# The last two operations of four weights' conversion, and the additions to k's sums, move from VectorE to GpSimd

## The chip, the cores and the metric

The kernel runs on one core of a Trainium2 chip. The metric is device time in microseconds (us) of one execution. The core has five engines that run their own instruction lists in order and wait for each other through semaphores: TensorE (PE in the rows), VectorE (DVE), ScalarE (ACT), GpSimd (POOL) and SyncE (SP, which here only issues transfers). An engine that waits for a semaphore holds everything that stands behind the waiting instruction in its list.

## The reference

Three layers follow each other: linear attention, a two-layer network, and a mixture of eight experts whose gate is balanced by eight Sinkhorn rounds.

```
k_s = exp(k - max(k, axis=seq));  k_s = k_s / (sum(k_s, axis=seq) + 1e-9)
q_s = exp(q - max(q, axis=dim));  q_s = q_s / (sum(q_s, axis=dim) + 1e-9)
x   = q_s @ (k_s^T @ v)                    # 4 batches, 8 heads, 576 tokens, 64 dims
x   = maximum(0.01*h, h) @ w_out,  h = x @ w_in        # 2304 x 512 -> 2048 -> 512
P   = exp(x @ w_gate - max), 8 rounds of row and column normalisation
out = sum_e P[:, e] * (relu(x @ w1[e]) @ w2[e])
```

The first network's two weights come as 64-bit floats. The kernel reads each as two 32-bit words and makes from them a high and a low fp32r part, so that three fp32r matmuls stand for one product of fp32 accuracy.

## The kernel before

Tokens lie in 18 tiles of 128 (`q_task(i)`, i from 0), which are grouped into 6 blocks of 384 (`x_task(bl)`, `first`, `second`). The hidden layer of the first network is cut into 16 units of 128 columns; a unit's weights have two halves, (u, 0) for the first matrix and (u, 1) for the second. `prep_half(u, half)` converts one half: it takes 512 numbers per partition through seven operations on VectorE and two on ScalarE, and the last two (lines 169 and 170) make the low part: L169 subtracts the high part, L170 adds the contribution of the low word and writes the result into `wa` (units 0 to 3), where the matmuls read it. In the kernel before, units 4 to 7 already do these two lines on GpSimd; all others do them on VectorE.

`k_task(b, hp)` handles batch b and pair of heads hp: VectorE takes the maximum (L269), ScalarE the exponential with its sum over the tokens in `sm` (L271), TensorE transposes (L279), ScalarE copies (L281), VectorE adds EPS to the sum (L282, 128 x 1) and takes the reciprocal (L283), TensorE multiplies by v, and ScalarE scales the product by the reciprocal (L295). `q_task` alternates between engines: maximum on VectorE (L305), subtraction on GpSimd (L307), exponential on ScalarE (L309), sum, addition and reciprocal on VectorE (L311 to L313), multiplication on GpSimd (L314), transposes on TensorE (L319) and a copy on ScalarE (L320). `x_task` multiplies the block by the batches' products (`px`), and writes the high part (ScalarE, L345) and the low part (VectorE, L346) of x into `xs`; `first(0)`, the matmuls `ph`, is the first use of them.

Everything is issued from a table of half steps: the tasks are generators, `at(t, task)` says in which half step one begins, and each half step advances all that are active by one piece. Steps below 0 lie ahead of `first(0)`. The lists of TensorE, ScalarE, GpSimd and SyncE are in the order in which the program text issues them, since they are set to be manual; only VectorE's list is put in order by the scheduler of the framework. The loads of the raw weights go round three buffers, so a load waits until L170 has read the buffer that it overwrites:

```
    for t, (u, half) in zip((-12, -8, -5, -1, 3, 6, 8, 11), halves0):
        at(t, prep_half, u, half)
```

`halves0` is (0,0), (1,0), (0,1), (1,1), (2,0), (3,0), (2,1), (3,1).

Of the kernel before, what the change touches and what calls it, by code (L numbers as in the profile page):

```python
# [16 lines left out]
EPS = 1e-9  # L17
# [5 lines left out]
def kernel(  # L23
# [26 lines left out]
    nc = tc.nc  # L50
# [12 lines left out]
    PU = 4  # L63
# [26 lines left out]
    def r32(ap):  # L90
        return ap.bitcast(F32)
# [26 lines left out]
    def unit(u):  # L118

        if (u // PU) % 2 == 0:  # L120
            t = wa[:, u % PU * US : (u % PU + 1) * US]
        else:
            t = later["wb"][:, u % PU * US : (u % PU + 1) * US]
        return t.rearrange("p (h l n) -> p h l n", h=2, l=2)
# [11 lines left out]
    def load(free=False):  # L136
        if queue[0][0] >= 2 * PU and not free:
            return
        u, half = queue.pop(0)
        t = raw_t[u, half] = later["ml"].tile([P, 2 * DM], F32, tag="raw", name=f"raw{u}_{half}", bufs=later["raws"])  # L140
        nc.sync.dma_start(
            t.bitcast(U32), wm[u, :, half * DM : (half + 1) * DM].bitcast(U32)
        )

    def prep_half(u, half):


        raw = raw_t.pop((u, half)).bitcast(U32).rearrange("p (n t) -> p n t", t=2)
        w0, w1 = raw[:, :, 0], raw[:, :, 1]
        hi, lo = unit(u)[:, half, 0, :], unit(u)[:, half, 1, :]  # L150
        a = later["ml"].tile([P, DM], U32, tag="ca", name=f"ca{u}_{half}", bufs=6 - later["raws"] if later["raws"] == 3 else 1)
        af, ef = a.bitcast(F32), w1.bitcast(F32)
        nc.scalar.activation(af, ef, AF.Abs)
        yield
        nc.vector.tensor_scalar(af, af, EXP_MIN, EXP_MAX, op0=ALU.max, op1=ALU.min)
        nc.vector.tensor_scalar(
            a, a, 3, 0x3FFFFFFF, op0=ALU.logical_shift_left, op1=ALU.bitwise_and
        )
        nc.vector.scalar_tensor_tensor(
            a, w1, 0xC0000000, a, op0=ALU.bitwise_and, op1=ALU.bitwise_or  # L160
        )
        yield
        nc.scalar.copy(hi, af)
        nc.vector.tensor_scalar(w1, a, 0xFF800000, None, op0=ALU.bitwise_and)
        nc.vector.scalar_tensor_tensor(ef, w0, 2.0**-52, ef, op0=ALU.mult, op1=ALU.mult)
        yield

        eng = nc.gpsimd if PU <= u < 2 * PU else nc.vector
        eng.tensor_tensor(af, af, r32(hi), op=ALU.subtract)  # L169
        eng.tensor_tensor(lo, af, ef, op=ALU.add)  # L170
        ready.add((u, half))
        if u < 2 * PU:
            load()
# [17 lines left out]
    def bank(name):  # L191
        pool, tag = spare[0]
        spare.append(spare.pop(0))
        return pool.tile([P, 512], F32, tag=tag, name=name)
# [8 lines left out]
    def mm(o, a, b, start, stop, **more):  # L203
        nc.tensor.matmul(o, a, b, start=start, stop=stop, **more)  # L204
# [60 lines left out]
    def k_task(b, hp):  # L265
        k = k_t.pop((b, hp))
        nm = att.tile([P, 1], F32, tag="knm", name=f"knm{b}_{hp}")
        sm = att.tile([P, 1], F32, tag="ksm", name=f"ksm{b}_{hp}", bufs=4)
        nc.vector.tensor_reduce(nm, k, axis=AX.X, op=ALU.max, negate=True)  # L269
        yield  # L270
        nc.scalar.activation(k, k, AF.Exp, bias=nm, accum_out=sm)  # L271
        yield PE_NEXT
        ke = att.tile([P, SC, P], F32, tag="ke", name=f"ke{b}_{hp}")
        for c0 in range(0, SC, 4):
            pt = bank(f"pk{b}_{hp}_{c0}").rearrange("p (c d) -> p c d", d=P)
            m = min(4, SC - c0)
            for c in range(c0, c0 + m):
                r = min(P, S - c * P)
                nc.tensor.transpose(pt[:r, c - c0, :], k[:, c * P : c * P + r], ident)  # L279
            r = min(P, S - (c0 + m - 1) * P)  # L280
            nc.scalar.copy(ke[:r, c0 : c0 + m, :], pt[:r, :m, :])  # L281
        nc.vector.tensor_scalar_add(sm, sm, EPS)  # L282
        nc.vector.reciprocal(sm, sm)  # L283
        yield PE_NEXT
        v = v_t.pop((b, hp))
        pt = bank(f"pkv{b}_{hp}")[:, :P]
        for c in range(SC):
            r = min(P, S - c * P)
            mm(pt, ke[:r, c, :], v[:r, c, :], c == 0, c == SC - 1)

        assert b < 2 or all(("x", i) in ready for i in range(-(-(b - 1) * S // P)))
        ready.add(("kv", b, hp))
        for j in range(2):
            js = slice(j * D, (j + 1) * D)
            nc.scalar.mul(kv[b % 2][js, hp, js], pt[js, js], sm[js])  # L295
# [981 lines left out]
    for b, tk, tv, ts in (  # L1277
# [4 lines left out]
    ):  # L1282
        for hp, t in enumerate(ts):
            if tk is not None:
                at(tk[hp], k_load, b, hp)
                at(tv[hp], v_load, b, hp)
            at(t, k_task, b, hp)
# [9 lines left out]
    for t, (u, half) in zip((-12, -8, -5, -1, 3, 6, 8, 11), halves0):  # L1297
        at(t, prep_half, u, half)
# [7 lines left out]
    for t, (f, half) in zip((26, 28, 32, 34, 36, 41, 43, 45), halves):  # L1306
        at(t, prep_half, PU + f, half)
    at(H2 + 2, open_raws)
    for ph in range(1, NPH - 1):
        for t, (f, half) in zip((5, 11, 16, 21, 28, 33, 39, 44), halves2):  # L1310
            at(H2 * ph + t - 3, load, True)
            at(H2 * ph + t, prep_half, PU * (ph + 1) + f, half)
# [108 lines left out]
```

## Time and profile before

| | before |
|---|---|
| median of 3 runs | 1951.55 us (1951.3 to 1952.67) |
| the profiled execution | 1952.44 us, of which the profile's span is 1950.7 us |
| TensorE busy | 1920.2 us (98%) |
| VectorE busy | 1550.5 us (79%) |
| ScalarE busy | 835.9 us (43%) |
| GpSimd busy | 754.8 us (39%) |
| TensorE's granted clock, mean | 0.995 of full |

Times in the rows are counted from the span's start. "Idle before" in square brackets is how long the engine had done nothing ahead of an instruction, and the arrow names what released it. Instructions of one line that follow each other are merged in the list in order of time, with their number behind an x.

### The profile page before, as it was taken

The numbers are of one execution on the slowest core, as the hardware profiler recorded it, in microseconds if no ns is written. First come the engines' busy times: TensorE is split into PE (matmuls) and PEld (weight loads), VectorE is DVE, ScalarE is ACT, GpSimd is POOL, SyncE is SP. The second block draws the span as 40 slices with busy tenths as digits, with TensorE's granted clock in tenths as the row PEclk, the third lists the DMA queues.
The fourth block names the chain that finished last, engine by engine and source line by source line (L and its number), as shares of the span: only waits on it lengthen the run. The fifth ranks groups of instructions, "written<-read, shape, count | busy, mean of one in ns | idle before, by whom it ended". The sixth has DMA issues, their size and how long they took to land.

```text
span 1950.7 us, 31219 instructions
## 1 busy us (share of the span) xinstructions
PE 1920.2 (98%) x10835; PEld 1862.6 (95%) x10835; DVE 1550.5 (79%) x2285; ACT 835.9 (43%) x1518; POOL 754.8 (39%) x560
## 2 busy tenths in 40 slices
PE   7999999999999999999999999999999999999998
PEld 6999999999888999899999999999999999999998
DVE  7866767756888787778897888888898888888886
ACT  6754434445544444333444333333344333333333
POOL 4134223123324333135434444445443444444442
PEclk8999999999999999999999999999999999999999
DMA  6502768657787988888788988788888888888884
GB/s 241 170 12 65 247 213 266 214 184 237 254 303 288 335 289 307 310 295 259 239 275 271 320 282 264 249 271 259 260 251 255 272 261 260 259 260 242 271 261 146
DMA packets 279450, 483.59 MB, mean 248 GB/s; under 512 B 23376, under 2 KB 62688, under 8 KB 279264
## 3 DMA queue, kind: packets, MB, share of 16 engines
q1 hardware_dynamic: 278496, 480.04, 74.6%
q0 software_dynamic: 800, 1.57, 0.5%
q8 instruction: 88, 1.44, 0.3%
q14 instruction: 66, 0.54, 0.1%
HBM read 356.14 MB, written 128.52 MB: 248 GB/s over the span
## 4 chain that ended last, share of the span: by engine, by line
PE 53%; DVE 4%; issue 0%; ACT 0%; DMA 0%; POOL 0%; SPq 0%; ACTq 0%; DVEq 0%; POOLq 0%
PE e L204 27%; PE pa L204 7%; PE pc L204 7%; PE pd L204 7%; PE pb L204 4%; DVE xs L539 1%; DVE c L944 1%; DVE mo_t L814 1%; DVE mo_t L800 1%; DVE wa L539 0%; PE po L914 0%; DVE acc L843 0%; DMA wa<-d 0%; POOL acc L838 0%; ACT xs L538 0%
## 5 line engine op out<-in xcount | busy, mean ns | idle before, releaser
L838 POOL TENSOR_TENSOR acc<-acc,acc 128x384 f32<-128x384 f32 x222 | 336.7, 1517 | 331.1 <-ACT acc L837 319.6
L204 PE MATMUL e<-xs,wb_t 128*128 128x384 f32 x1728 | 326.9, 335 | 4.2 <-DVE acc L843 2.5
L204 PEld LDWEIGHTS e<-xs,wb_t 128*128 128x128 f32 x1728 | 302.2, 188 | 4.9 <-DVE acc L843 2.9
L204 PE MATMUL e<-wa,wb_t 128*128 128x384 f32 x1464 | 278.3, 335 | 1.6 <-DVE wa L539 1.6
L204 PEld LDWEIGHTS e<-wa,wb_t 128*128 128x128 f32 x1464 | 256.5, 188 | 1.9 <-DVE wa L539 1.9
L814 POOL TENSOR_TENSOR mo_t<-mo_t 128x768 f32<-128x768 f32 x72 | 139.3, 1934 | 307.3 <-DVE mo_t L800 282.2
L837 ACT COPY acc<-e 128x384 f32<-128x384 f32 x222 | 106.5, 480 | 303.9 <-PE e L204 302.8
L539 DVE TENSOR_TENSOR wa<-mo_t,wa 128x768 fp32r<-128x768 f32 (+2 forms) x176 | 192.8, 1108 | 17.3 <-ACT wa L538 17.3
L539 DVE TENSOR_TENSOR xs<-mo_t,xs 128x768 fp32r<-128x768 f32 x145 | 164.9, 1153 | 25.5 <-ACT xs L538 25.5
L204 PE MATMUL pa<-xs,wb_t 128*128 128x384 f32 x888 | 181.4, 338 | 1.1 <-ACT c L997 1.1
L204 PE MATMUL pd<-xs,wb_t 128*128 128x384 f32 x888 | 178.9, 335 | 1.4 <-DVE xs L539 1.4
L538 ACT CAST wa<-mo_t 128x768 fp32r<-128x768 f32 (+2 forms) x176 | 143.8, 839 | 81.8 <-DVE mo_t L814 60.7
L204 PE MATMUL pc<-xs,wb_t 128*128 128x384 f32 x888 | 177.8, 334 | 0.0
L843 DVE TENSOR_TENSOR acc<-e,acc 128x384 f32<-128x384 f32 x284 | 145.4, 547 | 32.0 <-PE e L204 17.5
L204 PE MATMUL e<-wb_t,xs 128*128 128x512 f32 x720 | 167.7, 390 | 0.0
L204 PEld LDWEIGHTS e<-wb_t,xs 128*128 128x128 f32 x720 | 134.7, 188 | 27.3
L204 PEld LDWEIGHTS pa<-xs,wb_t 128*128 128x128 f32 x888 | 154.1, 188 | 6.7 <-ACT c L997 5.9
L204 PEld LDWEIGHTS pd<-xs,wb_t 128*128 128x128 f32 x888 | 155.7, 188 | 2.2 <-DVE xs L539 2.0
L204 PEld LDWEIGHTS pc<-xs,wb_t 128*128 128x128 f32 x888 | 156.0, 188 | 0.1
L538 ACT CAST xs<-mo_t 128x768 fp32r<-128x768 f32 x145 | 117.8, 835 | 84.0 <-DVE mo_t L814 64.4
L814 DVE TENSOR_TENSOR mo_t<-mo_t 128x768 f32<-128x768 f32 x80 | 146.0, 1826 | 0.0
L800 DVE SCALAR_TENSOR_TENSOR mo_t<-c,mo_t 128x768 f32<-128x768 f32 (+1 forms) x152 | 131.8, 888 | 2.5
(177 smaller groups left out, 3219.1 us busy)
## 6 DMA issues: line engine op xcount, KB each, us to landing
wb_t<-d SPq DMA_DIRECT2D x1050, 256.0 KB, 3.4
d<-wa SPq DMA_DIRECT2D x20, 1792.0 KB, 9.6
d<-wb_t SPq DMA_DIRECT2D x56, 512.0 KB, 4.5
mo_t<-in_w SPq DMA_DIRECT2D x40, 512.0 KB, 7.3
raw<-in_wm SPq DMA_DIRECT2D x32, 512.0 KB, 5.3
d<-wa SPq DMA_DIRECT2D x15, 1024.0 KB, 5.1
d<-xs SPq DMA_DIRECT2D x13, 768.0 KB, 4.9
d<-wb_t SPq DMA_DIRECT2D x9, 1024.0 KB, 5.0
```

What stands on the lines that cost most here:

```text
L204: nc.tensor.matmul(o, a, b, start=start, stop=stop, **more)
L538: nc.scalar.copy(hi, a)
L539: return lambda: nc.vector.tensor_tensor(lo, a, r32(hi), op=ALU.subtract)
L800: nc.vector.scalar_tensor_tensor(o, p, 0.0, r, op0=ALU.max, op1=ALU.mult)
L814: eng.tensor_tensor(raw_q(o), raw_q(x), raw_q(y), op=ALU.subtract)
L837: nc.scalar.copy(t, bk[b])
L838: nc.gpsimd.tensor_tensor(c22, c22, t, op=ALU.add)
L843: return nc.vector.tensor_tensor(a, bk[b], a, op=ALU.add)
L944: add = lambda o, x, y: nc.vector.tensor_tensor(o, x, y, op=ALU.add)
```

## The change

Two engines are exchanged. `prep_half` gives lines 169 and 170 of units 0 to 3 to GpSimd as well, and `k_task` gives its addition of EPS to GpSimd. The reciprocal behind that addition stays on VectorE.

```
@@ -165,7 +165,7 @@
-        eng = nc.gpsimd if PU <= u < 2 * PU else nc.vector
+        eng = nc.gpsimd if u < 2 * PU else nc.vector
         eng.tensor_tensor(af, af, r32(hi), op=ALU.subtract)
         eng.tensor_tensor(lo, af, ef, op=ALU.add)
@@ -279,7 +279,7 @@
-        nc.vector.tensor_scalar_add(sm, sm, EPS)
+        nc.gpsimd.tensor_scalar_add(sm, sm, EPS)
         nc.vector.reciprocal(sm, sm)
```

Sixteen instructions of L169 and L170 (eight halves) and sixteen of L282 change the engine. The lists of TensorE, ScalarE and SyncE stay as they were. The names in the lists below: `ca1_0` is the work tile of half (1, 0), `ksm1_3` the sum of batch 1 and pair of heads 3, `qmx2` and `qsm2` the maximum and the sum of token tile 2, `px0_2` the third product of token block 0; the number behind the last underscore is a buffer's.

The first place is GpSimd's list from the second instruction of token tile 0 to the multiplication of tile 1, some 14 to 20 us into the span.

```order
 L314 TENSOR_TENSOR acc0_79<-acc0_79,qsm0_208 128x512
+L169 TENSOR_TENSOR ca0_0_210<-ca0_0_210,wa_86 128x512
+L170 TENSOR_TENSOR wa_86<-ca0_0_210,raw0_0_177 128x512
 L307 TENSOR_TENSOR acc0_79<-acc0_79,qmx1_242 128x512
+L282 TENSOR_SCALAR ksm0_2_220<-ksm0_2_220 128x1
 L307 TENSOR_TENSOR acc0_79<-acc0_79,qmx2_282 128x512
+L282 TENSOR_SCALAR ksm0_3_240<-ksm0_3_240 128x1
 L314 TENSOR_TENSOR acc0_79<-acc0_79,qsm1_243 128x512
```

The pair of half (0, 0) now stands ahead of the subtractions of tiles 1 and 2, and the two additions stand between and behind those. At the same place VectorE's list is this now:

```order
L313 RECIPROCAL qsm0_208<-qsm0_208 128x8
L305 TENSOR_REDUCE qmx2_282<-acc0_79 128x8
L283 RECIPROCAL ksm0_2_220<-ksm0_2_220 128x1
L283 RECIPROCAL ksm0_3_240<-ksm0_3_240 128x1
L311 TENSOR_REDUCE qsm1_243<-acc0_79 128x8
```

The two reciprocals, which stood behind VectorE's own additions, now wait for GpSimd's, and the sum of tile 1 still stands behind them.

The second place is GpSimd's list some 30 to 38 us into the span, with the pair of half (1, 0).

```order
 L314 TENSOR_TENSOR acc1_80<-acc1_80,qsm3_313 128x512
+L169 TENSOR_TENSOR ca1_0_315<-ca1_0_315,wa_86 128x512
+L170 TENSOR_TENSOR wa_86<-ca1_0_315,raw1_0_195 128x512
 L307 TENSOR_TENSOR acc1_80<-acc1_80,qmx5_395 128x512
+L282 TENSOR_SCALAR ksm1_1_352<-ksm1_1_352 128x1
 L314 TENSOR_TENSOR acc1_80<-acc1_80,qsm4_355 128x512
 L314 TENSOR_TENSOR acc1_80<-acc1_80,qsm5_396 128x512
+L282 TENSOR_SCALAR ksm1_2_417<-ksm1_2_417 128x1
+L169 TENSOR_TENSOR ca0_1_419<-ca0_1_419,wa_86 128x512
+L170 TENSOR_TENSOR wa_86<-ca0_1_419,raw0_1_197 128x512
 L307 TENSOR_TENSOR acc2_81<-acc2_81,qmx6_473 128x512
 L307 TENSOR_TENSOR acc2_81<-acc2_81,qmx7_476 128x512
```

The addition for `ksm1_1` stands behind a pair and a subtraction now. The next instruction of this list, which is new too, is the addition for `ksm1_3`; it stands behind the pair of half (0, 1) and two subtractions. VectorE's list at the second place:

```order
 L311 TENSOR_REDUCE qsm4_355<-acc1_80 128x8
 L155 TENSOR_SCALAR ca0_1_419<-ca0_1_419 128x512
+L283 RECIPROCAL ksm1_1_352<-ksm1_1_352 128x1
 L312 TENSOR_SCALAR qsm4_355<-qsm4_355 128x8
+L156 TENSOR_SCALAR ca0_1_419<-ca0_1_419 128x512
+L313 RECIPROCAL qsm4_355<-qsm4_355 128x8
```

The reciprocal of `ksm1_1` moved behind the first operation of half (0, 1), and the sums of tile 4 stand behind it. VectorE's list at the third place, some 38 to 43 us into the span, before:

```order
L346 TENSOR_TENSOR xs_85<-px0_0_479,xs_85 128x384
L346 TENSOR_TENSOR xs_85<-px0_1_483,xs_85 128x384
L283 RECIPROCAL ksm1_2_417<-ksm1_2_417 128x1
L169 TENSOR_TENSOR ca0_1_419<-ca0_1_419,wa_86 128x512
L282 TENSOR_SCALAR ksm1_3_449<-ksm1_3_449 128x1
L170 TENSOR_TENSOR wa_86<-ca0_1_419,raw0_1_197 128x512
L346 TENSOR_TENSOR xs_85<-px0_2_514,xs_85 128x384
L346 TENSOR_TENSOR xs_85<-px0_3_518,xs_85 128x384
```

And in the changed kernel:

```order
L346 TENSOR_TENSOR xs_85<-px0_0_479,xs_85 128x384
L346 TENSOR_TENSOR xs_85<-px0_1_483,xs_85 128x384
L283 RECIPROCAL ksm1_2_417<-ksm1_2_417 128x1
L283 RECIPROCAL ksm1_3_449<-ksm1_3_449 128x1
L346 TENSOR_TENSOR xs_85<-px0_2_514,xs_85 128x384
L346 TENSOR_TENSOR xs_85<-px0_3_518,xs_85 128x384
```

The pair and the addition are gone from between the four L346, and the reciprocal of `ksm1_3` has come to stand ahead of the last two.

## Rows read from the trace of the kernel before

**Rows 1.** Busy us by stretch: PE, PEld, DVE, ACT, POOL, clock, DMA share, GB/s.
```profile
0.00:45.00 45.00, 31.38 (x173) 26.22 (x174) 33.22 (x78) 30.23 (x72) 18.16 (x23) 0.85 0.64 232
30.00:40.00 10.00, 7.04 (x41) 4.92 (x40) 10.00 (x23) 8.70 (x21) 6.72 (x7) 1.00 0.17 53
45.00:130.00 85.00, 85.00 (x540) 80.17 (x539) 63.13 (x142) 58.33 (x136) 22.95 (x21) 1.00 0.36 120
```

**Rows 2.** In order of time, all engines, 14 to 22 us: start, us, instruction.
```profile
14.00 0.69 DVE L169 TENSOR_TENSOR ca<-ca,wa 128x512 f32<-128x512 f32 x1
...
14.60 0.20 DVE L313 RECIPROCAL qsm<-qsm 128x8 f32<-128x8 f32 x1
...
14.95 1.37 POOL L314 TENSOR_TENSOR acc<-acc,qsm 128x512 f32<-128x512 f32 x1 [8.15 <-ACT kv L295]
...
16.28 2.04 POOL L307 TENSOR_TENSOR acc<-acc,qmx 128x512 f32<-128x512 f32 x2
...
18.01 0.69 DVE L311 TENSOR_REDUCE qsm<-acc 128x8 f32<-128x512 f32 x1 [1.68 <-ACT acc L309]
...
18.94 0.20 DVE L313 RECIPROCAL qsm<-qsm 128x8 f32<-128x8 f32 x1
...
21.07 0.78 ACT L271 ACTIVATE k<-k,knm 128x576 f32<-128x576 f32 x1 [3.09 <-DVE knm L269]
...
21.99 1.33 PE L279 MATMUL pk<-ident,k 128*128 128x128 f32 x5 [3.67 <-ACT k L271]
```

**Rows 3.** In order of time, VectorE, 28 to 43 us.
```profile
28.32 0.69 DVE L311 TENSOR_REDUCE qsm<-acc 128x8 f32<-128x512 f32 x1 [1.35 <-ACT acc L309]
...
30.27 0.19 DVE L313 RECIPROCAL qsm<-qsm 128x8 f32<-128x8 f32 x1
...
32.85 0.16 DVE L312 TENSOR_SCALAR qsm<-qsm 128x8 f32<-128x8 f32 x1
...
37.88 1.01 DVE L346 TENSOR_TENSOR xs<-px,xs 128x384 fp32r<-128x384 f32 x2
...
38.89 1.53 DVE L169 TENSOR_TENSOR ca<-ca,wa 128x512 f32<-128x512 f32 x1
40.34 0.14 DVE L282 TENSOR_SCALAR ksm<-ksm 128x1 f32<-128x1 f32 x1
...
41.79 1.01 DVE L346 TENSOR_TENSOR xs<-px,xs 128x384 fp32r<-128x384 f32 x2
```

**Rows 4.** In order of time, TensorE, 42 to 49 us.
```profile
42.48 0.63 PE L319 MATMUL pq<-ident,acc 128*128 128x128 f32 x4 [0.58 <-DVE xs L346]
...
44.79 4.41 PE L204 MATMUL ph<-xs,wa 128*128 128x384 f32 x24
```

**Rows 5.** L169 and L170 on GpSimd: ns min/median/max, first and last start.
```profile
L169 POOL TENSOR_TENSOR ca<-ca,wb_t x8: 1290/1620/1759, 142.1 to 189.1; 128x512 f32<-128x512 f32 x8
L170 POOL TENSOR_TENSOR wb_t<-ca,raw x8: 1299/1363/1372, 143.9 to 190.8; 128x512 fp32r<-128x512 f32 x8
```

**Rows 6.** In order of time, GpSimd, from the start and at 30 and 36 us.
```profile
0.35 0.10 POOL L1410 MEMSET const-uint8-127<- 128x1 uint8 x1
...
30.60 1.04 POOL L314 TENSOR_TENSOR acc<-acc,qsm 128x512 f32<-128x512 f32 x1 [2.07 <-DVE ksm L283]
...
36.37 1.05 POOL L314 TENSOR_TENSOR acc<-acc,qsm 128x512 f32<-128x512 f32 x1 [1.47 <-DVE qsm L313]
```

**Rows 7.** In order of time, ScalarE, TensorE and VectorE at 64 to 69 us.
```profile
64.45 0.62 ACT L163 CAST wa<-ca 128x512 fp32r<-128x512 f32 x1
...
66.99 2.54 PE L204 MATMUL ph<-xs,wa 128*128 128x384 f32 x12
...
67.41 1.15 DVE L346 TENSOR_TENSOR xs<-px,xs 128x384 fp32r<-128x384 f32 x2
```

**Rows 8.** Busy us by stretch, columns as in rows 1, around the clock's fall.
```profile
20.00:21.00 1.00, 0.00 (x0) 0.00 (x0) 1.00 (x3) 0.00 (x0) 1.00 (x2) 1.00 1.01 407
21.00:22.00 1.00, 0.01 (x1) 0.01 (x1) 1.00 (x2) 0.93 (x3) 0.33 (x1) 0.64 1.03 409
```

More of the change, by code (lines that the diff above doesn't have):

```diff
@@ L166, in prep_half @@
         yield
-        eng = nc.gpsimd if PU <= u < 2 * PU else nc.vector
+        eng = nc.gpsimd if u < 2 * PU else nc.vector
         eng.tensor_tensor(af, af, r32(hi), op=ALU.subtract)
@@ L281, in k_task @@
             nc.scalar.copy(ke[:r, c0 : c0 + m, :], pt[:r, :m, :])
-        nc.vector.tensor_scalar_add(sm, sm, EPS)
+        nc.gpsimd.tensor_scalar_add(sm, sm, EPS)
         nc.vector.reciprocal(sm, sm)
```

## The prediction

> **What bounds the kernel now.** I read the busy times by stretch first. In the first 45 us TensorE works 31.38 us; in the 85 us behind them it works all 85.00 [rows 1]. So the kernel is a start, in which TensorE waits for the attention's small operations, and then a dense row of matmuls. Whatever moves the first matmuls of the network (`ph`) moves everything behind them by as much, and a saving on VectorE later than that is hidden by TensorE's own work. The question is what the change does to the start.
>
> Then I read the start in order of time. From 14 to 22 us [rows 2] a chain goes round: VectorE's L313 of tile 0, GpSimd's L314 and two L307, ScalarE's exponential, VectorE's L311 of tile 1 (18.01, after 1.68 us idle), maxima, and at 21.07 ScalarE's exponential of batch 1, for which ScalarE had waited 3.09 us and TensorE 3.67. GpSimd is in that chain, though it is idle most of the time. From 30 to 40 us VectorE is busy all 10.00 us [rows 1]: the list runs from L311 at 28.32 to the last L346, which begin at 41.79 [rows 3]. TensorE waits for just those L346 ahead of `pq` at 42.48, and `ph` begins at 44.79 [rows 4], 3.0 us behind their begin.
>
> **The pieces and their prices.** Moved are eight pairs of L169 and L170 and sixteen L282. On VectorE a lone L169 took 0.69 us [rows 2]; beside busy GpSimd the pair took from 38.89 to 41.79, 2.9 us [rows 3]. On GpSimd the same lines, in the same shape, took 1.29 to 1.76 and 1.30 to 1.37 us [rows 5]; with 0.1 us between them (my estimate; L170 waits for L169) a pair is 2.7 to 3.2 us. I take 2.7 where VectorE stands still beside it and 2.9 where it works. The Trainium skill ("GPSIMD Engine Reference", section "Instruction dispatch") puts the floor of a two-input operation at some 2.5 cycles per element, with 1.2 GHz in section "Specifications": 512 elements would be an estimated 1.07 us, a pair 2.1, and three pairs on the path below would make the sum some 1.8 us smaller. The row of these very lines, 1.29 us at the least, decides, so I do not use it.
>
> An L282 on GpSimd has no row. Nearest below is a memset of 128 x 1 at 0.10 us [rows 6]; above I take twice VectorE's 0.14 [rows 3], the ratio that the pair has. I use 0.10, since size hardly matters here, and keep 0.28 for the range. From GpSimd to VectorE a hop of 0.15 (L313 ends at 14.80, L314 begins at 14.95) and a reciprocal of 0.20 [rows 2] follow: 0.35 together.
>
> What matters more is the place in the lists. Both engines keep their order: VectorE's reciprocals now wait for an L282 that stands in GpSimd's list behind a pair and one or two L307, and VectorE holds all that stands behind the reciprocal. Four places, each reckoned from the one ahead:
>
> *First, 18 us.* L313 of tile 0 no longer has an L169 ahead (0.60 us), but a reciprocal has moved ahead of it and its wait for L312 lies open: I count 0.4 of the 0.6, so L314 begins at 14.55 instead of 14.95 [rows 2]. It takes 1.05 [rows 6], to 15.6; the pair 2.7, to 18.3; L307 1.02 (half of 2.04), L282 0.10, L307 1.02, L282 0.10, to 20.55. With 0.35 the L311 of tile 1, which stands behind both reciprocals, begins at 20.9 instead of 18.01: 2.9 us late. ScalarE and TensorE, which waited for what follows anyway, are late by as much.
>
> *Second, 33 us.* L314 of tile 3 stood at 30.60 [rows 6]. It is 2.9 late, but VectorE needs 0.93 us from L311 to L313 where nothing lies between (18.01 to 18.94) and needed 1.95 here (28.32 to 30.27, with L169, L170 and an L282 between): 1.0 comes back. So 32.5; L314 1.04, pair 2.9, L307 1.02, L282 0.10: 37.55; with 0.35 it is 37.9. VectorE's L312 of tile 4, behind that reciprocal, stood at 32.85 [rows 3]: 5.1 late.
>
> *Third, 42 us.* L314 of tile 5 stood at 36.37 [rows 6]; with 5.1, and 0.3 since an L164 now stands ahead of its sum, it begins at 41.75. L314 1.05, L282 0.10, pair 2.7, two L307 2.04, L282 0.10: 47.75; with 0.35 it is 48.1. The last two L346 stood at 41.79: 6.3 late. What VectorE saves, the 2.9 us of the pair ahead of them, is inside that, as idle time. `ph` begins at 51.1 instead of 44.79.
>
> *Fourth, 68 us.* From `ph` on TensorE has no gaps to give back. Half (2, 0) gets its high part at 64.45 plus 0.62; a pair of 2.7, L282 and 0.35 end at 68.25, and the L346 behind that reciprocal stood at 67.41 [rows 7]: 0.85 late. The `ph` that reads them began at 66.99 and takes about 0.19 us for each of its 12 matmuls; it comes to this part at the eighth, 68.3, and the first L346 was done at about 67.95, so 0.35 is spare: 0.5 late.
>
> Past that, waits of the same kind fall on sums and halves with microseconds to spare, and I count them at nothing. The cover there is TensorE's own row of matmuls; if it were gone, the pair of half (1, 1), which the second set of matmuls behind `ph` reads, would be late next.
>
> **The sum.** 6.3 + 0.5 = 6.8 us. Against the profiled execution, 1952.44 us (a span of 1950.7 and 1.7 around it), that is 1959.2; the median of the runs shown is 0.9 lower, 1951.55, and so I predict 1958.3 us. Low ends (pairs of 2.6, 0.6 gained at the first place, the fourth hidden) take off 1.2, and if TensorE, whose transposes at 21.99 ran below the full clock [rows 8], is back at it earlier in the later start, up to 1.2 more: 4.4. High ends (pairs of 3.2: 1.3; five L282 of 0.28 on the path: 0.9; nothing gained at the first place: 0.4; no spare at the fourth: 0.35) give 9.8. The forecast's own range is 1955.9 to 1961.4.
>
> **The rivals.** *VectorE's relief wins.* From 28.32 to 42 us VectorE is the bound, and the change takes from it 1.0 us, 2.9 us and some 0.6 us of L282: 4.5 in all, 1947.0. That needs every L282 to be done before VectorE comes to the reciprocal; it decides where a pair and the L307 beside it take less time than VectorE has work ahead of the reciprocal. Against it: at the second place GpSimd needs 5 us behind L314, and VectorE's list has only three larger operations there. For it: GpSimd was busy 18.16 of the first 45 us [rows 1]. One in ten.
>
> *The first delay is hidden.* If batch 1's exponential at 21.07 really stood for a transfer, 2.9 us drop out: 3.9 are left, 1955.4. Against it the row names VectorE's maximum as what ended that wait [rows 2]. 15 in 100.
>
> *The clock falls.* At the second place TensorE loses its work: the products of block 0 need tile 2's copy, which stands on ScalarE behind the exponential of tile 5, and that waits for the delayed L307. By the times above TensorE has a gap of some 3 us ahead of the products and of 2 ahead of `pq`. Before, a gap of 3.67 us ended with the granted clock at 1.00 from 20 to 21 us and 0.64 from 21 to 22 [rows 8], on its way from 2.4 to 1.2 GHz. If it falls again just ahead of `ph`, the first two sets of `ph`, 4.41 us [rows 4], take up to twice as long: 2 to 4.4 us more, 3 in the middle, 1961.3. The Trainium skill ("TensorE: Matmul & The Clock Gate", section "What's actually happening") calls the lower level the default, which activity releases; by that rule the gaps speak for the fall, and the trace agrees with it for its one gap of 3.67 us. But the gaps here are shorter and broken by transposes. 17 in 100.
>
> *It does nothing that can be measured*, as the start is covered by something that I do not see: 3 in 100.
>
> **The numbers.** The forecast keeps 55 in 100. What a measurement of this kernel can tell from no change is about 0.2%, 3.9 us. Slower by more than that: the forecast, the clock, and a little of the case with the hidden delay, 0.74. Faster by more: 0.09 of the first rival. The same: 0.17, most of the hidden delay. The range leaves out the faster case and the nothing, and the far end of the clock's: 1953.5 to 1963.5.
>
> **What would show it.** In the profile after: `ph` begins at about 51 us; TensorE's busy time behind it is unchanged; VectorE stands idle ahead of three L283 (ahead of 21, 38 and 48 us), released by GpSimd's L282; GpSimd's pairs last 2.7 us and more, and the L307 of tiles 1, 5, 6 and 7 are late by 2 to 8 us. The forecast is wrong if those idle times are absent, if the pairs take near 2.1 us, or if TensorE, warm and late, catches up later in waits that I have taken for its own.

## The result and the profile after

The changed kernel takes 1961.99 us (median of 4 runs, 1961.11 to 1962.85) against 1951.42 us (4 runs, 1951.06 to 1952.67) before: 0.54% slower, with an interval of the ratio from 1.0042 to 1.0066. It was forecast at 1958.3 us, slower, with a range of 1953.5 to 1963.5 us. The profiled execution took 1961.37 us, its span 1959.6 us.

The busy times by stretch of the kernel after, which answer to [rows 1]:

```profile
0.00:45.00 45.00, 29.00 (x145) 24.43 (x146) 25.44 (x60) 27.30 (x64) 24.26 (x34) 0.81 0.61 222
45.00:130.00 85.00, 80.89 (x493) 74.31 (x492) 55.43 (x118) 56.30 (x133) 39.29 (x42) 0.98 0.38 125
```

In the start TensorE works 2.4 us less than before and VectorE 7.8 us less; GpSimd works 6.1 us more. The line that was not expected is the second: in the 85 us behind the start TensorE is no longer busy throughout, but 80.89 us, and its clock is at 0.98. (The start is longer now, so some of these 4.1 us still belong to it; from 55 to 140 us TensorE is busy 82.40 of 85 us, where it was busy all 85.00 before.)

The start in order of time, all engines, kernel after; first the place that answers to [rows 2]:

```profile
13.84 1.04 POOL L314 TENSOR_TENSOR acc<-acc,qsm 128x512 f32<-128x512 f32 x1 [3.43 <-DVE qsm L313]
...
14.84 1.27 POOL L169 TENSOR_TENSOR ca<-ca,wa 128x512 f32<-128x512 f32 x1
...
18.79 0.16 DVE L283 RECIPROCAL ksm<-ksm 128x1 f32<-128x1 f32 x1 [4.55 <-POOL ksm L282]
...
20.21 0.16 DVE L283 RECIPROCAL ksm<-ksm 128x1 f32<-128x1 f32 x1 [1.25 <-POOL ksm L282]
20.29 0.67 DVE L311 TENSOR_REDUCE qsm<-acc 128x8 f32<-128x512 f32 x1
...
24.20 1.11 PE L279 MATMUL pk<-ident,k 128*128 128x128 f32 x4 [6.94 <-ACT k L271]
```

VectorE stands idle for 4.55 and 1.25 us ahead of two L283 until GpSimd's L282 are done, which stand behind the pair and the L307. L311 of tile 1 comes at 20.29 instead of 18.01, the transposes at 24.20 instead of 21.99. At the prediction's second place VectorE is held for 2.47 us, and L312 of tile 4 comes at 36.90 instead of 32.85:

```profile
36.82 0.16 DVE L283 RECIPROCAL ksm<-ksm 128x1 f32<-128x1 f32 x1 [2.47 <-POOL ksm L282]
36.90 0.15 DVE L312 TENSOR_SCALAR qsm<-qsm 128x8 f32<-128x8 f32 x1
```

The same at the end of the start, which answers to [rows 3, 4]:

```profile
46.97 0.21 POOL L282 TENSOR_SCALAR ksm<-ksm 128x1 f32<-128x1 f32 x1
...
47.21 0.16 DVE L283 RECIPROCAL ksm<-ksm 128x1 f32<-128x1 f32 x1 [4.66 <-POOL ksm L282]
...
47.29 1.00 DVE L346 TENSOR_TENSOR xs<-px,xs 128x384 fp32r<-128x384 f32 x2
...
47.98 0.63 PE L319 MATMUL pq<-ident,acc 128*128 128x128 f32 x4 [1.51 <-DVE xs L346]
...
50.28 4.41 PE L204 MATMUL ph<-xs,wa 128*128 128x384 f32 x24
```

The last two L346 come at 47.29 instead of 41.79, `ph` at 50.28 instead of 44.79: 5.5 us late. VectorE's waits from 0 to 130 us (us in total, times, longest) say how much it stood for this. The second row, waits for a transfer of k, is taken up with the single pairs below:

```profile
DVE ksm L283 <- POOL ksm L282: 21.5, 8, 5.1
DVE knm L269 <- DMA k<-in_kt: 7.9, 3, 2.8
```

Behind `ph`, again in order of time, the delay grows twice more by little. The first row is the fourth place of the prediction:

```profile
74.26 1.16 PE L204 MATMUL ph<-xs,wa 128*128 128x384 f32 x5 [0.17 <-DVE xs L346]
...
85.52 0.16 DVE L283 RECIPROCAL ksm<-ksm 128x1 f32<-128x1 f32 x1 [1.23 <-POOL ksm L282]
...
87.41 1.57 PE L204 MATMUL pkv<-v,ke 128*128 128x128 f32 x10 [0.49 <-DVE hh L221]
```

`ph` is held for 0.17 us at 74.26 and reads the low part late; its followers are 5.9 us late instead of 5.5. A hold of L283 at 85.52 makes the subtraction for `hh` (L221) late, and TensorE waits for that: 6.6 us. Then, with the pair of half (3, 1):

```profile
108.17 0.16 DVE L283 RECIPROCAL ksm<-ksm 128x1 f32<-128x1 f32 x1 [5.12 <-POOL ksm L282]
...
110.25 0.55 DVE L221 TENSOR_TENSOR hh<-ph,hh 128x384 fp32r<-128x384 f32 x1
...
110.86 0.77 PE L279 MATMUL pk<-ident,k 128*128 128x128 f32 x5 [1.94 <-DVE hh L221]
...
111.46 2.24 PE L204 MATMUL pkv<-v,ke 128*128 128x128 f32 x10
...
113.63 3.13 PE L204 MATMUL ph<-xs,wa 128*128 128x384 f32 x12
```

Here two things happen. VectorE stands 5.12 us at L283, comes late to L305 and L221, and TensorE, whose transposes need what L221 sets free, has its largest gap behind `ph`: the transposes that began at 101.96 before begin at 110.86, 8.9 us late instead of 6.6. And then `pkv` takes 2.24 us instead of 1.47, `ph` 3.13 instead of 2.38, which was this row before:

```profile
103.91 2.38 PE L204 MATMUL ph<-xs,wa 128*128 128x384 f32 x12
```

The busy times by stretch say why (the last three numbers are the granted clock, the DMA share and GB/s):

```profile
110.00:112.00 2.00, 1.15 (x10) 1.15 (x11) 2.00 (x5) 0.40 (x1) 0.00 (x0) 0.97 0.02 2
112.00:114.00 2.00, 2.00 (x8) 1.55 (x8) 1.62 (x5) 0.60 (x3) 0.16 (x1) 0.50 0.00 0
114.00:116.00 2.00, 2.00 (x9) 2.00 (x9) 0.08 (x1) 0.99 (x3) 1.88 (x2) 0.68 0.01 4
```

The granted clock is at 0.50 from 112 to 114 us, 1.2 instead of 2.4 GHz, right behind the gap. From 116 us to beyond 500 us the delay is a constant 10.5 us. So the 10.6 us of the medians are, by TensorE's own instructions: 5.5 in the start, 0.4 at 68 us, 0.7 at 81, 2.3 in the gap at 102, and 1.6 by the fallen clock behind it (places in the time of the kernel before). The delay is still 10.4 us at 1866 us, but the two profiled executions end only 8.9 us apart, because 1.5 us are gained in the last 80 us. The run below in which only loads change places gains the same 1.5 us there against the same profile of before, so I take this for a difference between executions.

### The profile page after: what moved, and what is told of

It reads as the page before. It is cut to its first block, busy times and chain, and to the rows that moved or that the text cites. A ratio compares the mean times of both kernels' runs of the same rounds, so it can differ in the third digit from the quotient of the medians.

```text
span 1959.6 us, 31233 instructions
## 1 busy us (share of the span) xinstructions
PE 1923.4 (98%) x10835; PEld 1863.7 (95%) x10835; DVE 1540.2 (79%) x2253; ACT 836.5 (43%) x1518; POOL 778.5 (40%) x592
## 4 chain that ended last, share of the span: by engine, by line
PE 60%; DVE 5%; issue 1%; POOL 0%; ACT 0%; ACTq 0%; DVEq 0%; POOLq 0%
PE e L204 31%; PE pa L204 8%; PE pc L204 8%; PE pd L204 8%; PE pb L204 4%; DVE xs L539 1%; DVE c L944 1%; DVE mo_t L814 1%; DVE mo_t L800 1%; DVE wa L539 1%; DVE acc L843 0%; PE po L914 0%; POOL acc L838 0%; POOL mo_t L814 0%; ACT c L1025 0%
```

## The experiments

The theory is the prediction's: the time goes through VectorE's L283, which wait for L282 that stand behind a pair in GpSimd's list. The rivals are that the pairs do it by themselves, through other instructions behind them in that list, that the sums do it by themselves, or that VectorE's relief counts. (The letters of the rivals are each set's own; each text says what it means.) Executions of one kernel differ by some us, before from 1948.9 to 1955.4 over 27 runs, so medians tell 1 to 2 us, and the rest is read from the traces: I give how much later than in the profile of before TensorE begins the same instruction. Each kernel has one trace, and executions whose lists are the same up to 95 us differ by up to 1.1 us at `ph`, so less than that says nothing there.

**The two halves of the change, each alone.** First the pairs, with the sums on VectorE:

```
-        nc.gpsimd.tensor_scalar_add(sm, sm, EPS)
+        nc.vector.tensor_scalar_add(sm, sm, EPS)
```

> Both lines of units 0 to 3 on GpSimd, k's additions back on VectorE. Theory (the cost is VectorE held at a reciprocal whose addition stands behind a pair in GpSimd's list): the holds are gone; what is left is that GpSimd's subtractions of tiles 1 and 5 come later by a pair of 2.6 us, which moves ph by about 1.3 us: 1952.8 us (1952 to 1954), no idle time of VectorE that GpSimd ended, ph at about 46 us. Rival A (the pairs themselves are the cost, since GpSimd takes 2.6 us for what VectorE did in 1.4): most of the loss stays, 1958 us or more. Rival B (VectorE's relief is worth something by itself): 1948 to 1950 us.

1957.4 us (6 runs), ratio 1.0029 [1.0017, 1.0040], and the sum of the theory was 1952.8. No L283 waits for GpSimd here, and still `ph` is 3.9 us late. In order of time, 24 to 52 us:

```profile
35.31 0.63 ACT L309 ACTIVATE acc<-acc 128x512 f32<-128x512 f32 x1 [1.87 <-POOL acc L307]
...
37.88 2.93 PE L204 MATMUL px<-acc,kv 128*128 128x384 f32 x4 [2.87 <-ACT acc L320]
```

ScalarE's exponential waits for the L307 behind the pair of half (1, 0), so the copy behind it and the products `px` are late, by 2.6 us. `px` then takes 2.93 us, where it took 1.56:

```profile
38.00:40.00 2.00, 2.00 (x4) 1.09 (x5) 1.39 (x6) 1.67 (x4) 1.07 (x2) 0.50 0.00 0
...
42.00:44.00 2.00, 2.00 (x7) 1.39 (x6) 0.17 (x1) 1.06 (x4) 2.00 (x3) 0.57 0.23 23
```

The clock is at half, or near it, from 38 to 44 us. And at 102 us the gap is there as well, by another instruction:

```profile
104.98 0.69 DVE L305 TENSOR_REDUCE qmx<-acc 128x8 f32<-128x512 f32 x1 [4.62 <-POOL acc L307]
...
107.25 0.77 PE L279 MATMUL pk<-ident,k 128*128 128x128 f32 x5 [1.23 <-DVE hh L221]
```

L305 of the next token tile reads the block in which L307 writes, and waits for it nearly as long as L283 did.

Then the sums alone, with the pairs of units 0 to 3 on VectorE:

```
-        eng = nc.gpsimd if u < 2 * PU else nc.vector
+        eng = nc.gpsimd if PU <= u < 2 * PU else nc.vector
```

> Only k's additions on GpSimd, the pairs of units 0 to 3 on VectorE. Theory: the additions now stand behind subtractions of 1.04 us each, never behind a pair; the first hold near 18 us stays in part, ph comes about 1.3 us late, and near 100 us VectorE is held but early enough for TensorE: 1952.8 us (1951.5 to 1954.5). Rival A (pairs are the cost): 1951.4 us, no change. Rival C (an addition on GpSimd with the way there and back is slow by itself, whatever stands ahead of it): the 10.5 us stay for the most part, 1958 us or more.

1954.63 us (10 runs), ratio 1.0016 [1.0007, 1.0026], 0.1 us above the theory's range and 1.8 above its middle. L283 still waits 9.3 us for L282, now behind L307 and L314 alone; `ph` is 2.9 us late, where 1.3 was expected. By medians the halves cost 5.8 and 3.0 us, 8.8 of 10.6. For the sums the theory has the mechanism and too small a size; for the pairs it falls: they cost more than half by themselves.

**The holds taken away.** The addition of the change was issued right behind the exponential, ahead of the transposes:

```
         nc.scalar.activation(k, k, AF.Exp, bias=nm, accum_out=sm)
+        nc.gpsimd.tensor_scalar_add(sm, sm, EPS)
         yield PE_NEXT
```

> All that the change moved stays on GpSimd, but k's addition is issued right behind the exponential, a half step or two earlier, so that it stands ahead of most pairs in GpSimd's list. Theory (the place decides): ksm1_1, ksm1_3, ksm2_3, ksm3_2 and ksm3_3 no longer hold VectorE behind a pair; only ksm0_3 still stands behind one: 1953 to 1957 us, 1955 in the middle, with the gap of TensorE near 109 us gone. Rivals A and C (the work or the way to GpSimd is the cost): 1961 to 1962 us, as the change.

1960.28 us (5 runs), ratio 1.0043 [1.0029, 1.0057]: by medians 1.7 us less than with the whole change, with intervals that overlap, where the theory had 5 to 9 us. L283 waits 7.7 us instead of 21.5, but now GpSimd is the one that is held, and its L307 stand behind:

```profile
24.94 0.21 POOL L272 TENSOR_SCALAR ksm<-ksm 128x1 f32<-128x1 f32 x1 [4.66 <-ACT k L271]
```

`px` begins 5.9 us late, and the clock is at half from 36 to 46 us. The gap near 109 us, which was to go, is 1.15 us. An early place in an in-order list only moves the wait to that list.

Next, only the four additions of batch 3 back on VectorE, against the gap at 102 us:

```
-        nc.gpsimd.tensor_scalar_add(sm, sm, EPS)
+        (nc.vector if b == 3 else nc.gpsimd).tensor_scalar_add(sm, sm, EPS)
```

> The change, with the four additions of batch 3 alone back on VectorE. Theory: TensorE's gap near 109 us (2.3 us late) and the stretch of halved clock behind it (1.6 us) are both due to VectorE held for ksm3_2 and ksm3_3, so 3.9 us come back: 1958.1 us (1957.3 to 1959), and TensorE works without a gap and at full clock from 100 to 120 us. Rival D (that gap comes from GpSimd's late multiplications and subtractions of tiles 11 to 13, behind the pair of half (3, 1)): the gap stays, 1961 to 1962 us.

1961.73 us (4 runs), ratio 1.0053 [1.0038, 1.0068]; by time and by what holds VectorE the rival had it right.

```profile
108.34 0.69 DVE L305 TENSOR_REDUCE qmx<-acc 128x8 f32<-128x512 f32 x1 [4.60 <-POOL acc L307]
...
110.61 0.77 PE L279 MATMUL pk<-ident,k 128*128 128x128 f32 x5 [1.10 <-DVE hh L221]
```

As with the pairs alone, L305 takes the place of L283. TensorE loses 1.3 us here instead of 2.3, and the clock does not fall (1.00 from 100 to 118 us), but this execution was 0.9 us later at `ph` already, with lists that are the same up to 96 us. By its trace the delay behind 116 us is 8.7 us instead of 10.5, by the medians only 0.3 us came back; so what this edit is worth stays open between these, and it is not the theory's 3.9. When the pair of half (3, 1) is taken back as well:

```
+        eng = nc.gpsimd if u < 2 * PU and (u, half) != (3, 1) else nc.vector
```

> The change with two things of the stretch around 100 us undone together: the pair of half (3, 1) and the four L282 of batch 3 back on VectorE. Either alone is held to make VectorE late there. Revised theory: the gap ahead of the transposes at 102 us and the clock's fall behind it are gone, and the delay stays at the 6.6 us that it has before them: 1958.1 us (1957.2 to 1959.2 us). If the gap has another cause, or TensorE loses the same time later anyway: 1961 to 1962 us, as with the sums alone undone.

1959.2 us (5 runs), ratio 1.0037 [1.0024, 1.0050], at the upper end of the expected range. The sum of the busy times from 98 to 118 us:

```profile
sum 20.00, PE 20.00 PEld 18.85 DVE 14.48 ACT 14.61 POOL 8.31; mean PE 2.00 PEld 1.88 DVE 1.45 ACT 1.46 POOL 0.83
```

TensorE is busy for 20.00 of 20.00 us; the gap and the fall of the clock are gone, and the delay stays at the 7.6 us that it has at 82 us. It is 2.8 us less than with the whole change by medians; this execution began `ph` 1.1 us later than that of the change, from the first transposes on. The pair of half (3, 1) alone, on the kernel before:

```
+        eng = nc.gpsimd if PU <= u < 2 * PU or (u, half) == (3, 1) else nc.vector
```

> Before, with the pair of half (3, 1) alone on GpSimd and every sum on VectorE. Revised theory: behind this pair stand the L307 of tiles 12 and 13, for which VectorE's L305 and behind it the subtraction for hh wait; TensorE gets a gap of 1.0 to 1.6 us ahead of the transposes at 102 us, and nothing else moves: 1952.8 us (1952.0 to 1953.6 us). Rival F (each pair an equal share of 5.7 us): 0.7 us, 1952.1 us, without a gap there. Rival A: 1951 us or less.

1952.58 us (11 runs), before 1951.61, ratio 1.0005 [0.9996, 1.0014]: no difference by time. In the trace TensorE goes from 0.81 us early (the lists up to 95 us are those of before, so this is a difference between executions) to 0.02 late. Up to 500 us it does so at this very place and nowhere else, 0.8 us, with L305 waiting 4.60 us for L307. So the mechanism is shown, and its size alone is less than I had expected.

**The clock.** The pairs alone, and eight products of the identity in the gap ahead of `px`, whose result is overwritten:

```
+            if bl == 0 and c == 0:
+                for _ in range(8):
+                    mm(p[:, :P], ident, ident, True, True)
```

> The eight pairs on GpSimd, every sum on VectorE, and eight products of the identity with itself (128x128, their result overwritten) on TensorE in the gap of 2.87 us ahead of px. If the fallen clock from 38 to 44 us costs by itself: the granted clock stays at 1.00 there, px takes 1.56 instead of 2.93 us, ph begins 1.3 to 1.9 us earlier, 1955.8 us (1955.2 to 1956.4 us). If something else sets ph (VectorE, ScalarE): clock up, but still 1957.4 us. If the products themselves are in the way: 1958 us or more.

```profile
35.46 1.95 PE L204 MATMUL px<-ident 128*128 128x128 f32 x16
...
38.40 1.56 PE L204 MATMUL px<-acc,kv 128*128 128x384 f32 x4 [0.99 <-ACT acc L320]
...
48.88 0.75 DVE L269 TENSOR_REDUCE knm<-k 128x1 f32<-128x576 f32 x1 [5.44 <-DMA k<-in_kt]
...
54.33 2.21 PE L204 MATMUL y<-hh,wa 128*128 128x384 f32 x11 [1.53 <-DVE hh L221]
```

The clock stays at 1.00, `px` takes 1.56 us though it begins even later than in the pairs alone, and `ph` is 1.6 us late instead of 3.9. So 2.2 of those 3.9 us were the clock. "TensorE: Matmul & The Clock Gate" of the Trainium skill, section "What's actually happening", calls the lower level the default that activity releases; by that rule work in the gap keeps the clock up, and the trace agrees. But the median is 1958.88 us (5 runs), ratio 1.0038 [1.0026, 1.0051], no better than the pairs alone: VectorE waits 5.44 us for a transfer of k, L221 comes late, `y` waits 1.53 us, and what was won is lost by 57 us. The third expectation has the number, but not the reason, since `ph` comes earlier and not later; in the pairs alone the same L269 began at 48.34 after 2.66 us, so it is the transfer that sets when it can begin. The next runs show more of it.

**Single pairs.** Half (0, 1) alone on GpSimd:

```
+        eng = nc.gpsimd if PU <= u < 2 * PU or (u, half) == (0, 1) else nc.vector
```

> Before, with the pair of half (0, 1) alone on GpSimd and every sum on VectorE. Revised theory (a pair costs by what stands behind it in GpSimd's list): behind this pair stand only three L307 whose sums come 5 us later, so nothing is late, and VectorE has 2.9 us less ahead of the L346 for which pq waited 0.58 us: 1951.1 us (1950.3 to 1951.8 us). Rival F (a pair costs wherever it stands, the 5.7 us of the eight pairs shared out): 1952.3 us. Rival A (VectorE's relief counts in full): 1948.7 us.

1955.85 us (11 runs) against 1950.94, ratio 1.0022 [1.0013, 1.0031]. All three expectations of the time are wrong, though the first half of the theory's is right: `ph` begins 1.6 us earlier than before, of which up to 0.8 us may lie between executions.

```profile
38.26 1.29 POOL L170 TENSOR_TENSOR wa<-ca,raw 128x512 fp32r<-128x512 f32 x1
...
39.58 0.33 SPq L141 DMA_DIRECT2D raw<-in_wm  x1
...
40.00 0.86 SPq L253 DMA_DIRECT2D k<-in_kt  x2
...
43.22 4.41 PE L204 MATMUL ph<-xs,wa 128*128 128x384 f32 x24
...
45.48 0.75 DVE L269 TENSOR_REDUCE knm<-k 128x1 f32<-128x576 f32 x1 [5.25 <-DMA k<-in_kt]
...
50.93 2.21 PE L204 MATMUL y<-hh,wa 128*128 128x384 f32 x11 [1.34 <-DVE hh L221]
...
57.95 1.30 PE L204 MATMUL ph<-xs,wa 128*128 128x384 f32 x5 [1.81 <-DVE xs L346]
```

VectorE's list is put in order by the scheduler, and with two instructions gone from it the maximum L269 of batch 2 has come to stand ahead of the sums L311 (the piece of VectorE's list that differs; the names here lack the number of the batch or tile):

```
 L346 TENSOR_TENSOR xs<-px_3_518,xs 128x384
-L283 RECIPROCAL ksm_3_449<-ksm_3_449 128x1
+L269 TENSOR_REDUCE knm_0_739<-k_0_584 128x1
 L311 TENSOR_REDUCE qsm_474<-acc_81 128x8
```

Its k is loaded behind a `raw` that waits in SyncE's list until the pair has read its buffer (39.58); L269 can begin at 45.48 only. In the kernel before this `raw` went out later still, at 41.89, but there L269 stood behind the sums; so the order of VectorE's list is what is new, and not a later load. VectorE has waited 5.25 us by then and runs without a gap until it is late for `hh` and for the low part of x: TensorE waits 1.34 and 1.81 us. Behind the second wait the clock falls as well:

```profile
60.00:62.00 2.00, 2.00 (x9) 2.00 (x8) 0.56 (x1) 1.75 (x4) 0.00 (x0) 0.50 0.92 304
```

At 64 us TensorE is 3.5 us late: it has lost 1.5 and 1.9 us at the two waits and 1.6 us by the clock. In the whole change the same wait stands at 50.76 us (2.47 us, the second row of the waits above), but there `ph` is late enough to hide it. To take that wait away, the load of that `raw` was put behind the first two k of batch 2:

```
-            load()
+            owed.append(load) if (u, half) == (0, 1) else load()
-        nc.sync.dma_start(k_t[b, hp], kt[b, :, hp, :])
+        nc.sync.dma_start(k_t[b, hp], kt[b, :, hp, :]); owed and (b, hp) == (2, 1) and owed.pop()()
```

> Before with the pair of half (0, 1) alone on GpSimd, and the load of raw (3, 0), which waits for that half's L170, issued behind the loads of batch 2's first two k instead of ahead of them. Theory K (the pair alone cost time only because VectorE's list was written with the L269 of batch 2 ahead of the L311, and their k stands in SP's queue behind the raw that waits for the pair): k lands near 36 us, no L269 waits for it, ph begins 1 to 1.6 us earlier than before and keeps the lead: 1950 us (1949 to 1951.2 us). If VectorE has too much to do behind ph anyway: the lead is lost again, 1952 to 1956 us.

1952.48 us (11 runs), ratio 1.0003 [0.9994, 1.0011]; the second expectation had it. From 34 to 62 us no L269 waits for a load any more, and of the 5.0 us that TensorE lost between `ph` and 64 us it now loses 1.7, without a fall of the clock. But the scheduler has put another instruction ahead, an L305 that waits for q, and the lead of 0.8 us is lost all the same:

```profile
48.76 0.69 DVE L305 TENSOR_REDUCE qmx<-acc 128x8 f32<-128x512 f32 x1 [1.44 <-DMA acc<-in_q]
...
56.99 1.15 PE L204 MATMUL ph<-xs,wa 128*128 128x384 f32 x5 [1.67 <-DVE xs L346]
```

The same exchange of loads in the kernel before:

> Before, with the load of raw (3, 0) issued behind the loads of batch 2's first two k and nothing else changed. Theory K: the k of batch 2 is early, but no L269 waited for it before; two L269 of 0.74 us come to stand ahead of the L346 or the L311, so ph may begin up to 0.7 us later: 1951.5 us (1950.5 to 1952.5 us). If the early k is a gain of its own: 1950 us or less.

1951.14 us (11 runs), ratio 0.9998 [0.9990, 1.0007]: no difference, as expected. Early loads are no gain of their own; what half (0, 1) loses with the one order and not with the other comes from VectorE's wait for that k and what follows from it.

Half (1, 0) alone, the pair ahead of tile 5's L307:

```
+        eng = nc.gpsimd if PU <= u < 2 * PU or (u, half) == (1, 0) else nc.vector
```

> Before, with the pair of half (1, 0) alone on GpSimd and every sum on VectorE. Revised theory: this pair stands ahead of the L307 of tile 5, so ScalarE's exponential and px are 2.6 us late, TensorE's clock falls in that gap, and ph begins 3.4 to 3.9 us late: 1955.2 us (1954.2 to 1956.2 us), most of what the eight pairs cost. Rival F (each pair an equal share of 5.7 us): 1952.3 us. Rival A (VectorE is relieved of 1 us): 1950.6 us.

1952.82 us (11 runs), ratio 1.0013 [1.0004, 1.0022]. The mechanism is as expected (`px` waits 2.77 us, the clock is at 0.50 from 38 to 40 us), the size is not: VectorE, without this pair, brings L314 of tile 3 forward by 1.2 us, and `ph` is 1.5 us late, not 3.4 to 3.9.

**All pairs, behind the L307.** Five pairs are issued n operations of L307 or L314 later (the sums on VectorE, the bodies of the two lines unchanged; lines are shifted, L180 is the old L170, L174 the old L165):

```
+        n = {(0, 0): 4, (1, 0): 2, (0, 1): 3, (3, 0): 2, (3, 1): 2}.get((u, half), 0)
+        if n:
+            behind.append([n, last])
```

> All eight pairs on GpSimd, every sum on VectorE, but five pairs stand two to four GpSimd operations later in its list, behind the L307 and L314 that they stood ahead of. Revised theory: the subtractions are on time, px and the qmx maxima wait for no L307, the clock stays up: 1950.5 us (1949 to 1952 us), where the same pairs in their old places took 1957.4 us. Rival F (the pairs cost wherever they stand, through the late low parts, late loads or VectorE beside GpSimd): 1955 us or more. Rival A: 1947 us.

1955.18 us (9 runs), ratio 1.0021 [1.0012, 1.0031]. The revised theory is wrong on this one, and rival F had both the number and the reasons: `px` is on time (35.15), but two other costs come up.

```profile
36.31 1.50 POOL L180 TENSOR_TENSOR wa<-ca,raw 128x512 fp32r<-128x512 f32 x1
...
36.69 1.68 DVE L174 SCALAR_TENSOR_TENSOR raw<-raw 128x512 f32<-128x512 uint32 x1
...
39.60 2.86 PE L220 MATMUL px<-acc,kv 128*128 128x384 f32 x4 [1.91 <-DVE xs L364]
```

L174 on VectorE, which has two inputs, took 1.68 us beside GpSimd's L180 and the multiplication behind it, where the same line took 0.69 us beside an idle GpSimd (36.81 us in the run with half (1, 0) alone). GpSimd's two took 1.50 and 1.49 us, where they take some 1.3 and 1.04 alone. The "GPSIMD Engine Reference" of the Trainium skill, section "Specifications", lists SBUF interfaces that GpSimd shares with VectorE, with contention for VectorE's instructions with two inputs there; the trace agrees that the two slow each other. The L364 behind L174, which was L346, comes late, `px` waits 1.91 us for it and takes 2.86 us at a clock of 0.50 (40 to 42 us), and `ph` is 2.2 us late. And at 102 us the pair of half (3, 1), now behind the L307, is itself too late:

```profile
104.03 3.15 PE L220 MATMUL y<-hh,wa 128*128 128x384 f32 x10 [1.63 <-POOL wa L180]
```

`y` reads the low part and waits 1.63 us for it, and the clock falls to 0.51. Neither of the two places that were tried hides GpSimd's 2.6 us.

## Why the prediction was right, and what it missed

**The time.** 1961.99 us lies within the stated range, but 0.6 us above the forecast's own, 1955.9 to 1961.4. The stated range held because it had been widened for the clock, and the clock's 1961.3 comes near by luck: the clock did not slow the first `ph`, and of the 4.6 us that were missed (below) 3.0 are waits.

**The start** was right in its mechanism and near in its size. Predicted for L311 of tile 1, L312 of tile 4, the last L346 and `ph` were 20.9, 37.9, 48.1 and 51.1; measured 20.29, 36.90, 47.29 and 50.28. Most of the difference lies in where the chain begins: L314 of tile 0 came at 13.84, not 14.55. From L314 to L311 it took 6.45 us, predicted 6.35. A pair took 2.6 us (predicted 2.7 and 2.9), an L282 0.21 us (0.10, range to 0.28). The estimate of 1.07 us by the Trainium skill ("GPSIMD Engine Reference", section "Instruction dispatch"), which the prediction set aside for a row, is not met: the eight L169 took 1.29 us in the mean. But the runs show that the L283 are not the only way: at 36 and at 102 us they stand beside an L307 whose users, ScalarE's exponential and VectorE's L305, are held nearly as long (1.87 and 4.62 us with the pairs alone). Taking away one leaves the other.

That this start cost 0.8 us less than predicted shows little about its terms: the two runs whose lists are the same up to 96 us began `ph` 6.4 and 6.6 us late, against 6.3 predicted and 5.5 here.

**The fourth place**: 0.5 predicted, 0.4 measured.

**The step that failed** is the sentence "Past that, waits of the same kind fall on sums and halves with microseconds to spare, and I count them at nothing." They cost 0.7, 2.3 and, with the clock behind the gap, 1.6 us: 4.6 in all, against 3.8 us between the 6.8 predicted and the 10.6 measured, since the start gave 0.8 back in this execution. The trace of before had a row for it:

```profile
98.95 0.69 DVE L305 TENSOR_REDUCE qmx<-acc 128x8 f32<-128x512 f32 x1 [2.19 <-POOL acc L307]
...
100.62 0.54 DVE L221 TENSOR_TENSOR hh<-ph,hh 128x384 fp32r<-128x384 f32 x1
...
101.96 0.71 PE L279 MATMUL pk<-ident,k 128*128 128x128 f32 x5
```

L305 already waited 2.19 us for GpSimd there, with L221 four instructions behind it, which ended at 101.16, 0.8 us ahead of the transposes that need it. GpSimd's list at that place was to become 2.6 us longer.

**The rivals.** *VectorE's relief* is 1.6 us at `ph` at most (half (0, 1) alone; a run with the lists of before up to 95 us was 0.8 us early there too), and it is lost behind `ph`. *The first delay hidden* is out: the transposes behind it are 2.2 us late. *The clock* fell, but not just ahead of `ph`: once from 40 to 44 us (0.55 and 0.60), where in the whole change the held L346 hid it, and once at 112 us, where nothing did. What stays open is the share of the other five halves, which no run had alone, how the delay at 102 us divides between the sums and the pair of half (3, 1), and why the first transposes differ by up to 1.1 us between executions.

## What to carry to other kernels

An engine that is idle 60% of the time is not free: what counts is what stands behind the moved work in its in-order list, and who waits for that. Go through the waits that already name this engine as releaser, late ones too, and set the spare time of each against the length of the work moved in; a row with 2 us of waiting and 0.8 us of spare is a price, not a cover. Where a scheduler orders an engine's list, taking two instructions out puts others ahead, and one that waits for a transfer may be among them.

## What was not expected of the hardware

- TensorE's clock fell behind gaps of 1.94 us (at 110.86), 1.63 (at 104.03, pairs behind the L307), 1.81 (at 57.95, half (0, 1) alone) and 2.87 us (at 37.88, pairs alone) and not behind those of 1.10 and 1.23 us (at 110.61 and 107.25), 1.53 (at 54.33, with the eight products) and 1.67 us (at 56.99, with the loads exchanged). So the length of the gap does not tell it by itself: 1.63 and 1.67 us went either way. Behind that of 2.87 us it stayed low for some 6 us of work, which cost 2.2 us, nearly as much as the gap.
- A 128 x 1 addition took 0.21 us on GpSimd in the median, and 0.14 on VectorE.
- L165 (L174), with two inputs, took 0.69 us beside an idle GpSimd and 1.68 us beside GpSimd's L180 and L331, a multiplication, which took 1.50 and 1.49 us.
